# Softcap attention and spectral mixing: who issues the transfers that move squares between partitions

## Chip, cores and metric

The kernel runs on one core of one Trainium2 chip. The metric is the device time of one execution in microseconds; lower is better. Several executions are timed and their median is told. One more execution was recorded by the hardware profiler; every row below is from that one.

## The reference, cut to what matters

```python
scores = scale * np.matmul(q, k.transpose(0, 1, 3, 2))      # 8 batches, 12 heads, 448 x 64
scores = cap * np.tanh(scores / cap)
attn = softmax(scores)                                      # with 1e-09 added to the sum
x = (attn @ v) laid out as [8, 448, 768]

theta = x @ w_theta
zr, zi = x * np.cos(theta), x * np.sin(theta)
y = einsum('ts,bsd->btd', w_tok_r, zr) + einsum('ts,bsd->btd', w_tok_i, zi)
u = x + y
return u + np.maximum(u @ w_ch, 0.0)
```

The theta product and the last product sum over the 768 channels, and the product with `w_tok` sums over the 448 tokens. TensorE sums over partitions, so between the first and the second of them the values `zr` and `zi` must be turned round: channels stand on partitions before, tokens after.

## The kernel before, in words

All work is laid out by hand. `pipeline` runs one script of short words per attention stage `s` (two pairs of heads each, three stages per batch), and each word calls one function. The scripts `FRONT`, `PARTS` and `OTHER` fix the order on every engine; nothing is reordered later, and each engine works through its own instructions in that order. The attention of a batch runs beside the spectral part of the batch before it. A batch `b` of the spectral part takes the three scripts of `PARTS` (a first, a second and a third script); the last batch is finished by scripts of its own in `OTHER`, where no attention is left.

Products that need float32 accuracy are made of three TensorE products in a shorter format: a value is split into a high part (a cast on ScalarE, ACT) and a low part (a subtraction on VectorE, DVE). For the mixing over tokens these are `z_high` (word `h`, L502, writes `zh`) and `z_low` (word `l`, L509, writes `zl`); `mix` (word `M`, L519 to L521, writes `mx`) multiplies them.

The turning is done in two steps. `flip` (word `f`, L481) transposes 32x32 blocks in place of their partitions on DVE and writes a tile `f`, which in the trace is called `g_row` where it lies in a fixed row of memory. `carry` (word `D`, L485 to L493) then moves blocks between partitions with sixteen transfers of 32 partitions x 448 values, 56 KB each, from `f` to a new tile `t`. There are three carries a batch, D0, D1 and D2, each for two of the six channel blocks. D0 and D1 stand in the first script and D2 in the second, in this order of words (cut):

```
... f0 f1 D0 N d2 e2 T3 y3 Pa0 S3 Pb0 q1 t3 e3 d3 a1a a1b sc1 T4 y4 d4 T5 y5 d5 r2 r3 f2 f3 D1
... h0a l0a h0b l0b W h1a ... M0a l1a r4 h1b M0b r5 l1b f4 f5 D2 e0 h2a M1a l2a e1 M1b h2b l2b m0 I ...
    ... M3a h4a l4a M3b h4b l4b Pa0 m2 w2 S3 q1 t3 M4a ...
```

The first word that reads D0's tile is `h0a`, D1's is `h2a`, D2's is `h4a` (in the script `... u0 e2 u1 a0b M3a h4a l4a M3b h4b l4b ...`); the product of the last is `M4a`. A `z_high` reads columns from all four column blocks of `t` and all partitions, so it waits for all sixteen transfers of its carry.

Two things tie the carries together. In the batches with full scripts the tile `f` has one fixed room (`FLIP = (1,)`), so the flips for D2 (`f4 f5`) may not write before D1's sixteen transfers have read it and ended. And the transfers are issued by two engines' queues: SyncE (SP), whose queue also loads `q` and `k` (L232), broadcasts the reciprocal sums (word `I`, `bc`, L407) and stores the output, and GpSimd (POOL), which in this part of the program does nothing else.

Which engine issues what is the line that the change touches; `d` is one of the four column blocks of `t`, `m` one of the four groups of 32 partitions, and `b` counts the batches from 0.

Of the kernel before, what the change touches and what calls it, by code (L numbers as in the profile page):

```python
# [75 lines left out]
def softcap_attn_then_spectral_mix(ctx, tc, qk2, v, cap, w_theta, w_tok, w_ch, outT):  # L76
    nc = tc.nc
    B, NP, P, _, S = qk2.shape
# [406 lines left out]
    def carry(b, i):  # L485

        Z[b, i, "t"] = large.take([P, 4 * S], F32, f"t{b}_{i}")
        f, t = Z[b, i, "f"], Z[b, i, "t"]
        for m in range(4):
            for d in range(4):  # L490
                queue = nc.gpsimd if (b < B - 1 or i) and d == 3 else nc.sync
                queue.dma_start(t[32 * m : 32 * m + 32, d * S : (d + 1) * S], f[32 * d : 32 * d + 32, m * S : (m + 1) * S])  # L492
        large.give(Z.pop((b, i, "f")))  # L493

# [70 lines left out]
    def pipeline(general):  # L565
# [5 lines left out]
        def run(s, b, word):  # L571
# [44 lines left out]
            elif word == "v":  # L616
                if live:
                    load_v(s)
            elif name == "q":
                for part in range(2):  # L620
                    if s + 1 < WHOLE or s + 1 == WHOLE and (i, part) != (1, 1):
                        load_raw(2 * s + 2 + i, part)
            elif word == "Pa1":
                prep_q(2 * s + 1)
            elif word == "Pb1":
                prep_k(2 * s + 1)
            elif word == "Pa0":
                prep_q(2 * s + 2)
            elif word == "Pb0":
                prep_k(2 * s + 2)  # L630
            elif name == "w":
                weights(WEIGHTS.get((s, i), ""))
            elif name == "u":
                split_x(b, i, "us")
            elif name == "X":
                if b + 1 < B:
                    split_x(b + 1, i, "xs")
            elif name == "Y":
                split_x(b, i, "xs")
            elif name in ("h", "l", "M"):  # L640
                {"h": z_high, "l": z_low, "M": mix}[name](b, i, half)
            else:
                {"T": theta, "y": turns, "d": reduce, "sc": sincos, "r": rotate, "f": flip, "D": carry, "m": mix_out, "C": chan,
                 "c": chan_out}[name](b, i)
# [70 lines left out]
```

## Time and profile before

| | |
|---|---|
| Timed, median of 3 runs | 909.82 us (907.93 to 910.62) |
| Profiled execution, its time | 907.38 us |
| Profiled execution, its span | 905.5 us |
| PE (TensorE products) busy | 892.0 us, 99% of the span |
| DVE busy | 657.3 us, 73% |
| ACT busy | 572.3 us, 63% |
| POOL busy | 53.1 us, 6% |
| Carry transfers issued by SP in the line changed | 292 |
| Carry transfers issued by POOL in the line changed | 92 |

The span is the time from the first to the last instruction; the execution's own time is 1.9 us more. Busy shares are means over the whole span; PE's busy time is made of overlapping pipelined products, so even at 99% single waits can lie between them. A chain of waits shows, step by step, what released the work that ended last.

### The profile page before, as it was taken

How to read it: one execution, taken by the hardware profiler on the slowest of the kernel's cores; microseconds unless marked ns; L12 is line 12 of the kernel's file. 1: busy time of each engine (PE TensorE's matmuls, PEld its weight loads, DVE VectorE, ACT ScalarE, POOL GpSimd, SP SyncE). 2: the span in 40 equal slices, each digit the busy share in tenths (PEclk: the TensorE clock that was granted, in tenths of full speed). 3: DMA queues.
4: the chain of work that ended last, by engine and by line, in shares of the span. 5: the costliest groups of instructions: out<-in, count | busy, mean ns of one | idle time of the engine just before them, and what ended most of it. 6: DMA issues, size and time to landing. Idle time of an engine off the chain costs nothing.

```text
span 905.5 us, 13212 instructions
## 1 busy us (share of the span) xinstructions
PE 892.0 (99%) x4896; PEld 638.5 (71%) x4896; DVE 657.3 (73%) x1095; ACT 572.3 (63%) x633; POOL 53.1 (6%) x109
## 2 busy tenths in 40 slices
PE   8999999999999999999999999999999999999997
PEld 4235575757758668677686686776876867779996
DVE  6899859969866598675985678855986659765741
ACT  6887865569845597547965488545894459733420
POOL 0000111100100011000100000000010000100100
PEclk9999999999999999999999999999999999999999
DMA  7653373442423325222442233333242331410411
GB/s 267 203 187 86 101 176 108 149 130 55 123 71 93 92 56 158 63 82 72 105 120 66 79 89 114 82 92 92 71 120 55 112 92 52 110 44 25 111 40 64
DMA packets 51947, 90.70 MB, mean 100 GB/s; under 512 B 10913, under 2 KB 44833, under 8 KB 51873
## 3 DMA queue, kind: packets, MB, share of 16 engines
q1 hardware_dynamic: 44592, 69.21, 26.8%
q0 software_dynamic: 3824, 9.61, 4.0%
q10 hardware_dynamic: 3456, 10.95, 3.9%
q8 instruction: 40, 0.66, 0.3%
q14 instruction: 35, 0.28, 0.1%
HBM read 45.68 MB, written 11.01 MB: 63 GB/s over the span
## 4 chain that ended last, share of the span: by engine, by line
PE 72%; DVE 16%; SPq 3%; issue 3%; DMA 3%; ACT 3%; DVEq 0%; ACTq 0%
PE s L278 11%; PE a L362 10%; PE ch L431 7%; PE ch L433 6%; PE ch L432 6%; PE mx L521 5%; PE th L431 5%; PE mx L519 4%; PE th L432 4%; PE mx L520 4%; PE th L433 4%; PE r L389 3%; SPq L492 3%; DVE g_row L481 2%; DMA t<-g_row 2%
## 5 line engine op out<-in xcount | busy, mean ns | idle before, releaser
L305 ACT ACTIVATE p<-s,qscale 128x1792 f32<-128x1792 f32 (+1 forms) x77 | 117.0, 1520 | 102.9 <-PE s L278 93.3
L519 PE MATMUL mx<-wtk_h,zh 128*128 128x448 f32 x336 | 125.1, 372 | 3.9 <-ACT zh L502 3.9
L521 PE MATMUL mx<-wtk_h,zl 128*128 128x448 f32 x336 | 123.9, 369 | 1.0 <-DVE zl L509 0.6
L520 PE MATMUL mx<-wtk_l,zh 128*128 128x448 f32 x336 | 123.0, 366 | 0.0
L318 ACT ACTIVATE p<-p,cap_sb 128x1792 f32<-128x1792 f32 (+1 forms) x77 | 119.9, 1559 | 2.6 <-PE a L362 1.9
L431 PE MATMUL th<-xs,wth_h 128*128 128x448 f32 x288 | 107.5, 373 | 0.0
L431 PE MATMUL ch<-us,wch_h 128*128 128x448 f32 x288 | 107.4, 373 | 0.0
L432 PE MATMUL th<-xs,wth_h 128*128 128x448 f32 x288 | 105.5, 366 | 0.0
L433 PE MATMUL ch<-us,wch_l 128*128 128x448 f32 x288 | 105.5, 366 | 0.0
L432 PE MATMUL ch<-us,wch_h 128*128 128x448 f32 x288 | 105.3, 366 | 0.0
L433 PE MATMUL th<-xs,wth_l 128*128 128x448 f32 x288 | 105.3, 365 | 0.0
L362 PE MATMUL a<-p,v 128*64 128x448 f32 x496 | 102.6, 545 | 0.0
L362 PEld LDWEIGHTS a<-p,v 128*64 128x64 f32 x496 | 33.1, 136 | 63.9 <-issue 62.5
L519 PEld LDWEIGHTS mx<-wtk_h,zh 128*128 128x128 f32 x336 | 63.1, 188 | 19.1 <-ACT zh L502 7.4
L492 POOL DMA_DIRECT2D t<-g_row x76 | 38.5, 513 | 588.8 <-DVE x_row L414 156.7
L502 ACT CAST zh<-t 128x512 fp32r<-128x512 f32 x84 | 44.6, 560 | 41.6 <-DMA t<-g_row 12.4
L521 PEld LDWEIGHTS mx<-wtk_h,zl 128*128 128x128 f32 x336 | 63.1, 188 | 9.6 <-DVE zl L509 4.4
L520 PEld LDWEIGHTS mx<-wtk_l,zh 128*128 128x128 f32 x336 | 63.1, 188 | 5.1
L431 PEld LDWEIGHTS th<-xs,wth_h 128*128 128x128 f32 x288 | 54.1, 188 | 14.2 <-issue 5.1
L431 PEld LDWEIGHTS ch<-us,wch_h 128*128 128x128 f32 x288 | 54.1, 188 | 13.6 <-issue 2.9
L509 DVE TENSOR_TENSOR zl<-t,zh 128x512 fp32r<-128x512 f32 x84 | 50.1, 616 | 16.7 <-ACT zh L502 9.4
L535 DVE SCALAR_TENSOR_TENSOR x<-ch,x 128x448 f32<-128x448 f32 x43 | 26.7, 622 | 48.3 <-PE ch L433 48.3
(517 smaller groups left out, 1563.5 us busy)
## 6 DMA issues: line engine op xcount, KB each, us to landing
t<-g_row SPq DMA_DIRECT2D x228, 56.0 KB, 2.0
k<-in_qk SPq DMA_DIRECT2D x47, 224.0 KB, 3.4
v<-in_v ACTq DMA_DIRECT2D x23, 448.0 KB, 3.3
out_dram<-x SPq DMA_DIRECT2D x43, 224.0 KB, 1.9
q<-in_qk SPq DMA_DIRECT2D x42, 224.0 KB, 2.8
bc<-ri SPq DMA_DIRECT2D x68, 112.0 KB, 2.3
t<-g_row POOLq DMA_DIRECT2D x76, 56.0 KB, 2.1
x_row<-ri SPq DMA_DIRECT2D x24, 112.0 KB, 2.3
```

The source lines that it names most:

```text
L278: nc.tensor.matmul(out[:, h, :S], kk[rows], qq[rows], start=m == 0, stop=m == len(products) - 1)
L305: nc.scalar.activation(pp, spt.pop((s, n))[:, :m, :, :S], AF.Tanh, scale=qscale)
L318: nc.scalar.activation(pp, pp, AF.Exp, scale=cap_sb)
L362: nc.tensor.matmul(acc_of["a", s, i][h * D : (h + 1) * D, :S], vt[s][:, 6 * i + 3 * h + c, :], U[s, (i, c)][:, h, :], start=first and c == ...
L431: nc.tensor.matmul(acc[:, :S], wh[:, j, ms], t[:, 0, :], start=j == 0, stop=False)
L432: nc.tensor.matmul(acc[:, :S], wh[:, j, ms], t[:, 1, :], start=False, stop=False)
L433: nc.tensor.matmul(acc[:, :S], wl[:, j, ms], t[:, 0, :], start=False, stop=j == NJ - 1)
L492: queue.dma_start(t[32 * m : 32 * m + 32, d * S : (d + 1) * S], f[32 * d : 32 * d + 32, m * S : (m + 1) * S])
L509: nc.vector.tensor_tensor(zl, tokens(b, j)[:, c0:c1], zh.bitcast(F32), op=ALU.subtract)
L519: nc.tensor.matmul(acc[:, :S], zh, wtk_h[:, c, :], start=c == 0, stop=False)
L520: nc.tensor.matmul(acc[:, :S], zh, wtk_l[:, c, :], start=False, stop=False)
L521: nc.tensor.matmul(acc[:, :S], zl, wtk_h[:, c, :], start=False, stop=c == NC2 - 1)
```

## The change

From the second batch on (`b` of 1 and above) POOL issues the transfers with `d` of 2 and 3 instead of those with `d` of 3 alone. Eight of the sixteen transfers of a carry then go through POOL's queue and eight through SP's, where it was four and twelve. The first batch stays as it was (four and twelve), and so does the first carry of the last batch (all sixteen on SP). It is 20 carries of the 24 and 80 transfers that change their queue. What is moved, and from where to where, stays.

```diff
-                queue = nc.gpsimd if (b < B - 1 or i) and d == 3 else nc.sync
+                queue = nc.gpsimd if (b < B - 1 or i) and d >= (2 if b else 3) else nc.sync
```

In SP's queue in the second batch (names `t_0`, `t_1`, `t_2` are the tiles of D0, D1 and D2; `bc` the broadcasts, `q`, `k` and `x_row` loads) the order around the carries is this:

```order
-L492 DMA t_0_1743<-g_row 32x448 x12
+L492 DMA t_0_1743<-g_row 32x448 x8
 L232 DMA k_1804<-in_qk 128x448
-L492 DMA t_1_1871<-g_row 32x448 x12
+L492 DMA t_1_1871<-g_row 32x448 x8
 L232 DMA q_1956<-in_qk 128x448
 L232 DMA x_row<-in_qk 128x448
 L232 DMA k_1963<-in_qk 128x448
-L492 DMA t_2_1995<-g_row 32x448 x12
+L492 DMA t_2_1995<-g_row 32x448 x8
 L407 DMA bc_0_2046<-ri_2041 64x448 x2
 L407 DMA bc_1_2049<-ri_2041 64x448 x2
```

Each group of twelve became eight, and what stands behind it in the queue is the same. In POOL's queue the same three carries, and those of the third batch, stand after one another; this is the order of the changed kernel:

```order
L135 DMA swc5b_raw<-in_wch 128x768
L492 DMA t_0_1743<-g_row 32x448 x8
L492 DMA t_1_1871<-g_row 32x448 x8
L492 DMA t_2_1995<-g_row 32x448 x8
L492 DMA t_0_2668<-g_row 32x448 x8
L492 DMA t_1_2796<-g_row 32x448 x8
L492 DMA t_2_2920<-g_row 32x448 x8
```

Where it read x4 it reads x8, and nothing stands between the carries. On ACT, the first cast that reads D2's tile in the second batch waits for the semaphores of the transfers (DMAHW those of SP and ACT, DMASW those of POOL):

```order
-L502 CAST zh_1915<-t_2_1995 128x512 [waits DMAHW2_49,DMAHW1_49,DMAHW3_49,DMAHW0_49,DMAHW4_49,DMASW7_49,DMAHW5_49,DMASW2_49,DMAHW6_49,DMASW1_49,DMAHW7_49,DMASW0_49,PE_49]
+L502 CAST zh_1915<-t_2_1995 128x512 [waits DMAHW0_49,DMASW7_49,DMAHW1_49,DMASW6_49,DMAHW2_49,DMASW5_49,DMAHW3_49,DMASW4_49,DMAHW4_49,DMASW3_49,DMAHW5_49,DMASW2_49,DMAHW6_49,DMASW1_49,DMAHW7_49,DMASW0_49,PE_49]
```

It waited for twelve DMA semaphores and now for sixteen. On PE, DVE and ACT no instruction is added, taken away or moved.

## Rows read from the trace of the kernel before

**Rows 1.** The page, first part: busy time, share of the span, instructions.

```profile
PE 892.0 (99%) x4896; PEld 638.5 (71%) x4896; DVE 657.3 (73%) x1095; ACT 572.3 (63%) x633; POOL 53.1 (6%) x109
```

**Rows 2.** Busy time by stretch: length, PE, PEld, DVE, ACT, POOL; clock; DMA share; GB/s.

```profile
214.06:322.64 108.58, 107.28 (x596) 79.30 (x596) 78.25 (x127) 71.36 (x79) 6.19 (x12) 1.00 0.32 90
322.64:429.63 106.99, 106.99 (x596) 79.39 (x597) 78.23 (x127) 71.52 (x79) 6.12 (x12) 1.00 0.33 91
429.63:537.57 107.94, 107.57 (x596) 79.23 (x598) 78.11 (x127) 71.32 (x79) 6.12 (x12) 1.00 0.33 90
537.57:645.70 108.13, 107.37 (x596) 79.28 (x598) 78.23 (x127) 71.33 (x79) 6.00 (x12) 1.00 0.32 90
645.70:754.34 108.64, 107.30 (x596) 79.31 (x597) 78.02 (x127) 71.41 (x79) 5.91 (x12) 1.00 0.32 90
822.00:899.72 77.72, 77.72 (x382) 71.55 (x382) 39.49 (x63) 23.33 (x37) 3.92 (x8) 1.00 0.22 61
```

**Rows 3.** PE's timeline at D2's first product, second and third batch: start, length.

```profile
251.37 0.37 PE L278 MATMUL s<-q17l,k17h 64*128 64x448 f32 x2
252.98 0.47 PE L519 MATMUL mx<-wtk_h,zh 128*128 128x448 f32 x1 [1.25 <-ACT zh L502]
...
359.93 0.38 PE L278 MATMUL s<-q23l,k23h 64*128 64x448 f32 x2
360.24 0.47 PE L519 MATMUL mx<-wtk_h,zh 128*128 128x448 f32 x1
```

**Rows 4.** ACT's timeline: casts of D0, D1, D2 (second batch), D2 (third).

```profile
226.78 1.54 ACT L502 CAST zh<-t 128x512 fp32r<-128x512 f32 x3
...
239.55 0.62 ACT L502 CAST zh<-t 128x512 fp32r<-128x512 f32 x1 [1.24 <-DMA t<-g_row]
...
252.31 1.03 ACT L502 CAST zh<-t 128x512 fp32r<-128x512 f32 x2 [4.81 <-DMA t<-g_row]
...
359.05 1.04 ACT L502 CAST zh<-t 128x512 fp32r<-128x512 f32 x2 [2.98 <-DMA t<-g_row]
```

**Rows 5.** SP's queue, second batch, D0, D1, D2: start, time over the group.

```profile
214.06 8.02 SPq L492 DMA_DIRECT2D t<-g_row  x12
...
230.13 7.49 SPq L492 DMA_DIRECT2D t<-g_row  x12
...
241.82 8.77 SPq L492 DMA_DIRECT2D t<-g_row  x12
```

**Rows 6.** L492 by queue: issue ns min/median/max; landing us min/median/max (SP, then POOL).

```profile
L492 SPq DMA_DIRECT2D t<-g_row x228: 507/588/1642, 214.1 to 863.2; - x114
L492 POOL DMA_DIRECT2D t<-g_row x76: 496/496/716, 214.7 to 858.5; - x76
DMA to landing us min/median/max: 1.9/2.0/5.4
DMA to landing us min/median/max: 1.8/2.1/4.5
```

**Rows 7.** Waits of DVE, 205 to 800 us; then its timeline, second batch.

```profile
DVE g_row L481 <- DMA t<-g_row: 14.9, 6, 2.9
...
239.58 2.10 DVE L481 STREAM_TRANSPOSE g_row<-z 128x896 f32<-128x896 f32 x2 [2.37 <-DMA t<-g_row]
...
249.59 1.08 DVE L342 TENSOR_TENSOR ps<-ps,g_row 64x896 f32<-64x896 f32 x1
252.96 1.16 DVE L509 TENSOR_TENSOR zl<-t,zh 128x512 fp32r<-128x512 f32 x2 [2.29 <-DMA bc<-ri]
```

**Rows 8.** POOL's timeline at D1 of the second batch.

```profile
230.68 0.50 POOL L492 DMA_DIRECT2D t<-g_row  x1 [13.84 <-DVE g_row L481]
231.47 1.62 POOL L492 DMA_DIRECT2D t<-g_row  x3 [0.29 <-issue]
```

**Rows 9.** Busy time by stretch (columns as in rows 2), while D1 is issued.

```profile
338.63:346.10 7.47, 7.47 (x46) 5.88 (x42) 6.05 (x10) 7.43 (x7) 1.98 (x4) 1.00 0.59 170
```

**Rows 10.** Semaphore waits ahead of L502, 214 to 800 us: ns min/median/max.

```profile
L502 ACTq EVENT_SEMAPHORE  x144: 17/38/3785, 223.8 to 794.6; - x144
```

## The prediction, made before the changed kernel ran

> **What bounds the kernel now.** I read the busy shares first [rows 1]: PE is busy 892.0 us, 99% of the span, every other engine under 75%. So time can only be won where PE waits, and the change touches no PE instruction. Next I cut the span into the steady batches, each from the first transfer of its D0 to that of the next batch, and compared them [rows 2]. The second to the sixth batch hold the same work (596 products each), but they last 108.58, 106.99, 107.94, 108.13 and 108.64 us. In the third (106.99) PE is never idle; in the others it idles 1.30, 0.37, 0.76 and 1.34 us. That is the reading to learn here: one batch shows what the schedule costs without waits, and what the others take more is 1.59 + 0.95 + 1.14 + 1.65 = 5.33 us.
>
> Who is waited for? In the second batch the last score product starts at 251.37 and the first mixing product of D2's tile at 252.98, 1.61 us later, with a wait for ACT's cast of `zh`; in the third batch the same two stand 0.31 us apart [rows 3]. So PE stood 1.30 us for the cast that reads D2. ACT started that cast at 252.31 after 4.81 us of idleness that ended with a landing; in the third batch it idled 2.98 us at the same place [rows 4]. The cast waits for the last of D2's sixteen transfers. SP took 8.77 us to issue its twelve there, from 241.82 on [rows 5]; POOL has only four.
>
> One step further back, DVE idles 14.9 us in six times before a flip, for landings [rows 7]: D2's flip starts at 239.58 after 2.37 us of waiting, because it overwrites the tile that D1's transfers read. D1's twelve on SP ran from 230.13 over 7.49 us [rows 5], so the last was issued near 230.13 + 7.49 - 0.59 = 237.03 and landed about 2.0 us later [rows 6], at 239.0; ACT's cast of D1 (239.55) and the flip (239.58) follow [rows 4, 7]. So two carries lie in series on this path, D1 and then D2, and SP's issuing is most of each.
>
> **The change, part by part.** *SP loses four transfers per carry.* Twelve took 7.49 us [rows 5], 0.624 us each. With eight the last is issued 7 x 0.624 = 4.4 us after the first instead of 6.9, and lands at +6.4 instead of +8.9 us.
>
> *POOL gains four.* It starts 0.55 us after SP (230.68 against 230.13) [rows 5, 8]. Its interval is (1.62 - 0.50) / 2 = 0.56 us within the three, and (231.47 + 1.62 - 230.68 - 0.50) / 3 = 0.64 with the pause of 0.29 us [rows 8]. The eighth is issued at 0.55 + 7 x 0.56 to 0.64, that is +4.5 to +5.0 us, and with the median landing of 2.1 us [rows 6] is there at +6.6 to +7.1. POOL does nothing else in these batches, so nothing queues behind.
>
> *Sixteen transfers in a shorter time.* While D1 is issued the DMA engines are busy 0.59 of 7.47 us [rows 9], which is 4.4 us of work; squeezed into 5.0 us that is 0.88. No row shows the landing at that load. The bounds are the median, 2.1 us, and POOL's longest, 4.5 us [rows 6], with which the carry is complete at 4.5 + 4.5 = +9.0, no earlier than now. I take +7.2 for D1 and +6.7 for D2, nearer to the median, because most transfers are issued off that peak: D1 lands 1.7 us earlier, D2 takes 2.2 us less.
>
> *What follows.* D2's flip was waiting 2.37 us [rows 7], so it moves up by all of the 1.7 us. D2's transfers then start 1.7 us earlier and take 2.2 us less: the cast may start 3.9 us earlier. ACT has 4.81 us of idleness before it [rows 4], so nothing holds it. DVE's subtraction for the same product starts at 252.96 after 2.29 us of idleness; the work before it ends at 249.59 + 1.08 = 250.67 [rows 7], and earlier flips only pull that forward. PE's wait was 1.30 us, so both are in time with a microsecond or more to spare. Next late at that place is PE itself.
>
> *More waits.* ACT's cast and DVE's flip now wait for sixteen DMA semaphores and not twelve. A wait takes 38 ns [rows 10], so 0.15 us on engines that sit idle there: nothing on the path. If that cover were gone it would be 0.15 us in each of two carries a batch, 2 us over seven.
>
> *Places without gain.* D0's cast starts at 226.78 with no idle time before it [rows 4], some 3 us after the last landing (214.06 + 8.02 - 0.59 + 2.0 = 223.5) [rows 5, 6]; ACT's own order hides D0. In the last batch PE is busy all 77.72 us from 822.00 on [rows 2], so D1 and D2 there win nothing. The first batch is unchanged. The seventh runs into other scripts and has no twin to compare it with; I count nothing for it.
>
> **The sum**, against the profiled execution of 907.4 us: four batches come down to the third one's length, 907.4 - 5.3 = 902.1 us. The timed runs have a median of 909.8, 2.4 us above the profiled one. Waits of this kind vary from batch to batch (0 to 1.65 us), so part of those 2.4 us may be of this kind and go too. I add a third: **902.8 us**, 0.8% less than the median.
>
> **A page against the rows.** SP's issuing is 7.49 us and a landing 2.0 us [rows 5, 6]: here the issuing is the long part. The Trainium skill, "DMA: Bandwidth & Descriptors", section "Issuing engines are not separate DMA queues", says that issuing from several engines only saves the sequencer's issue time, "which is usually small relative to the DMA itself". By that rule the change would bring next to nothing, about 907 to 910 us; these rows speak against the word small here.
>
> **Rivals.**
> *No measurable difference.* The transfers hold each other up: sixteen at a load of 0.88 land so much later that a carry ends as before. It needs landings of 8.9 - 4.5 = 4.4 us for POOL's last, against a median of 2.1 and a longest of 4.5; for it speaks that SP landed one as late as 5.4 [rows 6]. Then the flip and the cast stay where they are: 907.4 to 909.8 us. Halfway, with landings near 4.0 us, each carry gains 0.4 and the two 0.8 us of the 0.95 to 1.65 in four batches: 3.2 us, 904.2 us.
>
> *Slower: POOL becomes the late queue.* With eight to issue, POOL decides as soon as its interval is over (8.9 - 2.1 - 0.55) / 7 = 0.9 us. At 1.0 us instead of 0.56 to 0.64 a carry lands at 0.55 + 7.0 + 2.1 = +9.6, 0.7 us later than now; D1 and D2 add up to 1.4 us per batch. In the third batch the product would follow the cast by 252.98 - 252.31 = 0.67 us, at 359.05 + 0.67 = 359.7, and PE came at 360.24 [rows 3, 4], so 0.5 us are spare there. Second, fourth to sixth and seventh batch lose 1.4 us and the third 0.9: 7.9 us, 915 to 918 us. Against it: none of POOL's 76 transfers took over 716 ns to issue [rows 6]. What could do it is DVE holding GpSimd off for whole instructions of about 1.1 us. The Trainium skill, "SBUF — State Buffer", section "SBUF: two separate sides", states such a trap: GpSimd writes the descriptors of its transfers itself and is locked out while VectorE runs some copies. By that rule this rival is what would happen; the median landing of POOL's transfers, 0.1 us above SP's, shows little of it.
>
> **How the numbers follow.** About 0.3%, 2.7 us, is what a measurement of this kernel can tell from no change. The forecast (PE's waits for D2 gone, 900.8 to 905.5) has 0.71, no difference through crowded transfers 0.13, half gains (up to 907.5) 0.07, a late POOL 0.09. Faster is the forecast and most half gains, 0.76; same 0.15; slower 0.09. The range goes from 900.5, the sum with a microsecond and a half of room, to 908.0, which takes in the half gains and the start of the second case.
>
> **What will show it.** Right, if SP's groups at L492 read x8 and about 5 us and POOL's x8 and 4 to 5 us; if DVE's wait at the flip and ACT's before the D2 cast shrink by about 2 and 4 us; if PE's wait for `zh` in the steady batches is gone; and if all five of them last about 107.0 us. Wrong, if POOL's group takes over 6 us, if landings grow to 4 us and more, or if PE waits elsewhere in those batches.

## The result, and the profile after

The changed kernel takes 901.17 us (median of 6 runs, 900.24 to 901.78), the kernel before 907.88 us beside it (6 runs, 906.68 to 910.62): 0.9919 of the time, with an interval of 0.9906 to 0.9933. The forecast was 902.8 us. The profiled execution took 901.09 us with a span of 899.2, 6.3 us less than before.

The first line of the page, and the first line of the chain that ended last, after and then before:

```profile
PE 889.7 (99%) x4896; PEld 639.2 (71%) x4896; DVE 657.6 (73%) x1095; ACT 572.4 (64%) x633; POOL 92.0 (10%) x189
...
PE 93%; DVE 3%; ACT 1%; issue 1%; DMA 1%; SPq 0%; ACTq 0%
```

```profile
PE 72%; DVE 16%; SPq 3%; issue 3%; DMA 3%; ACT 3%; DVEq 0%; ACTq 0%
```

POOL's busy time grew from 53.1 us [rows 1] by 38.9, which is 80 transfers of 0.49 us; nothing else moved by more than 2.3. The chain runs over PE for 93% of the span, where it was 72%, and SP's queue, at 3% before, has no share in it worth a per cent.

The busy times by stretch, from the first transfer of a batch's D0 to that of the next (columns as in [rows 2]: length, PE, PEld, DVE, ACT, POOL, clock, DMA share, GB/s); the sixth row is the seventh batch:

```profile
213.57:320.55 106.98, 106.98 (x596) 79.39 (x596) 78.33 (x127) 71.45 (x79) 11.89 (x24) 1.00 0.32 91
320.55:427.56 107.01, 107.01 (x596) 79.41 (x598) 78.16 (x127) 71.33 (x79) 11.97 (x24) 1.00 0.32 91
427.56:534.54 106.98, 106.98 (x596) 79.39 (x598) 78.06 (x127) 71.43 (x79) 11.79 (x24) 1.00 0.33 91
534.54:641.55 107.01, 107.01 (x596) 79.35 (x598) 78.16 (x127) 71.30 (x79) 11.97 (x24) 1.00 0.31 91
641.55:748.51 106.96, 106.96 (x596) 79.40 (x597) 78.17 (x127) 71.32 (x79) 11.98 (x24) 1.00 0.32 91
748.51:828.97 80.46, 80.46 (x427) 63.06 (x428) 58.45 (x94) 48.94 (x64) 11.88 (x24) 1.00 0.24 64
```

In all six length and PE are equal: PE never waits. The five steady batches together go from 540.28 us [rows 2] to 534.94, which is 5.34 us less. The seventh batch, from the first transfer of its D0 to that of the eighth, goes from 81.23 to 80.46 us, 0.77 less. What lies ahead of the second batch's D0 is 0.49 shorter (213.57 against 214.06), the end from the eighth batch's D0 on 0.30 longer. The sum is 6.30 us, the whole difference of the spans.

The place where PE waited, D2's first product in the second batch [rows 3], and ACT's casts of D1 and D2 and DVE's flip there [rows 4, 7]; three timelines, of PE, ACT and DVE:

```profile
250.89 0.37 PE L278 MATMUL s<-q17l,k17h 64*128 64x448 f32 x2
251.19 0.47 PE L519 MATMUL mx<-wtk_h,zh 128*128 128x448 f32 x1
```

```profile
236.05 1.79 ACT L318 ACTIVATE p<-p,cap_sb 128x1792 f32<-128x1792 f32 x1
237.96 0.62 ACT L502 CAST zh<-t 128x512 fp32r<-128x512 f32 x1
...
248.25 1.03 ACT L502 CAST zh<-t 128x512 fp32r<-128x512 f32 x2 [1.22 <-PE mx L521]
```

```profile
238.09 2.10 DVE L481 STREAM_TRANSPOSE g_row<-z 128x896 f32<-128x896 f32 x2 [1.35 <-DMA x_row<-in_qk]
```

The product follows the score product after 0.30 us, where it was 1.61 [rows 3]. ACT's cast of D2 starts 2.9 us ahead of it. Its row names PE as what ended the wait, but D2's last transfer landed at 247.92, 0.33 us before the cast, much as before (251.94 and 252.31), so the landing may still be what it waits for. D1's cast has no idle time in brackets: it follows the work before it on ACT. The flip still waits for transfers, 1.35 us instead of 2.37 [rows 7]. Its row names a load (`x_row`), yet it starts 0.6 us after D1's last landing as it did before (238.09 after 237.48, 239.58 after 239.01), and still does in a run below that moves those loads away (238.84 after 238.23).

SP's and POOL's queues in the same batch (D0, D1, D2):

```profile
213.57 4.99 SPq L492 DMA_DIRECT2D t<-g_row  x8
...
229.64 4.96 SPq L492 DMA_DIRECT2D t<-g_row  x8
...
240.33 6.02 SPq L492 DMA_DIRECT2D t<-g_row  x8
```

```profile
214.24 4.12 POOL L492 DMA_DIRECT2D t<-g_row  x8 [44.71 <-PE s L278]
230.17 0.50 POOL L492 DMA_DIRECT2D t<-g_row  x1 [11.81 <-DVE g_row L481]
230.87 3.42 POOL L492 DMA_DIRECT2D t<-g_row  x7 [0.20 <-issue]
240.86 4.01 POOL L492 DMA_DIRECT2D t<-g_row  x8 [6.57 <-DVE zl L509]
```

SP's twelve took 8.02, 7.49 and 8.77 us [rows 5]; its eight take 4.99, 4.96 and 6.02. POOL's interval within D1's seven is (3.42 - 0.50) / 6 = 0.49 us, and its eighth goes out at 230.87 + 2.92 - 229.64 = +4.15 us from SP's first.

The transfers of L492 by queue over the whole span, landing us (min/median/max), SP and then POOL:

```profile
DMA to landing us min/median/max: 1.9/2.6/5.4
DMA to landing us min/median/max: 1.8/2.3/5.0
```

The median landing rose from 2.0 to 2.6 us on SP and from 2.1 to 2.3 on POOL [rows 6]: the crowding is real, but small beside the issuing that was saved.

### The profile page after: what moved, and what is told of

Read it like the earlier page. It is cut to its first block, busy times and chain, and to the rows that moved or that the text cites. A ratio compares the mean times of both kernels' runs of the same rounds, so it can differ in the third digit from the quotient of the medians.

```text
span 899.2 us, 13310 instructions
## 1 busy us (share of the span) xinstructions
PE 889.7 (99%) x4896; PEld 639.2 (71%) x4896; DVE 657.6 (73%) x1095; ACT 572.4 (64%) x633; POOL 92.0 (10%) x189
## 4 chain that ended last, share of the span: by engine, by line
PE 93%; DVE 3%; ACT 1%; issue 1%; DMA 1%; SPq 0%; ACTq 0%
PE s L278 15%; PE a L362 12%; PE mx L519 7%; PE mx L520 7%; PE th L431 7%; PE mx L521 7%; PE ch L431 7%; PE th L432 7%; PE th L433 7%; PE ch L433 6%; PE ch L432 6%; PE r L389 4%; PE a L355 2%; ACT p L305 1%; DVE wch_l L161 0%
## 5 line engine op out<-in xcount | busy, mean ns | idle before, releaser
L492 POOL DMA_DIRECT2D t<-g_row x152 | 75.4, 503 | 544.4 <-DVE x L414 153.0
L461 DVE SCALAR_TENSOR_TENSOR z<-z 128x448 f32<-128x448 f32 x48 | 29.7, 619 | 42.0 <-ACT z L456 41.9
```

## The experiments

The theory: PE waits for the last transfer of D2, behind D1 and D2 in series, and SP's issuing is most of each. Its rivals: that transfers hold each other up, that POOL becomes late, and that the gain comes from SP's queue being free sooner for its loads. All kernels are the changed kernel with one edit or two, and ratios are to the kernel before, run on the same chip. "D1 at +7.9" means: its last transfer lands 7.9 us after its first was issued, computed from the trace's issue and completion records.

**One carry at a time.** The three runs split every carry but one as before. The line is shown against the kernel before:

```diff
-                queue = nc.gpsimd if (b < B - 1 or i) and d >= (2 if b else 3) else nc.sync
+                queue = nc.gpsimd if (b < B - 1 or i) and d >= (2 if b and i == 0 else 3) else nc.sync
```

This is for D0 alone; the other two have `i == 1` (D1) and `i == 2` (D2).

> Eight and eight for D0 alone, from the second batch on; D1 and D2 as before (twelve and four). My theory (PE waits for D2, which waits for D1 and D2 in series, and D0 lands 3 us before it is read): no difference, ratio 0.998 to 1.002, second to sixth batch together 538 to 542 us as before. Rival (what counts is SP's queue being free earlier for the loads and broadcasts behind every carry): a third of the gain, ratio 0.997 or less.

> Eight and eight for D1 alone. Theory: D1 lands about 1.1 us earlier, D2's flip and with it all of D2 moves up by as much, so most of the 1.3 us waits go: 902 to 904 us, ratio 0.993 to 0.996; PE idle in the five steady batches together 0 to 1 us where it was 3.8. Rival (D1 is hidden, only D2's own issuing counts): ratio 0.998 to 1.002.

> Eight and eight for D2 alone. Theory: D2's own issuing is 2.3 us shorter, more than the longest wait of 1.3 us, so nearly the whole gain: 901 to 902.5 us, ratio 0.991 to 0.994; PE not idle in the steady batches. Rival (the gain is the sum of shares of the three carries): a third to a half of the gain, ratio 0.995 to 0.997.

D0 alone: 907.36 us, ratio 1.0002 (0.9989 to 1.0014), no change. D1 alone: 902.78, ratio 0.9938 (0.9919 to 0.9958). D2 alone: 902.94, ratio 0.9944 (0.9927 to 0.9962). The five batches by stretch with D0 alone:

```profile
213.56:321.61 108.05, 107.29 (x596) 79.32 (x596) 78.25 (x127) 71.42 (x79) 7.99 (x16) 1.00 0.32 90
321.61:428.60 106.99, 106.99 (x596) 79.42 (x598) 78.25 (x127) 71.55 (x79) 8.06 (x16) 1.00 0.33 91
428.60:536.84 108.24, 107.58 (x596) 79.23 (x596) 78.21 (x127) 71.32 (x79) 8.08 (x16) 1.00 0.33 90
536.84:644.15 107.31, 107.29 (x596) 79.28 (x598) 78.12 (x127) 71.43 (x79) 7.89 (x16) 1.00 0.32 91
644.15:752.45 108.30, 107.29 (x596) 79.31 (x596) 78.22 (x127) 71.34 (x79) 7.96 (x16) 1.00 0.32 90
```

PE still idles 0.66 to 1.01 us in three of the five and 0.02 in a fourth, although SP is done with D0 sooner. The five are 1.4 us shorter together than before [rows 2]; but D2, which is split as before, landed sooner in the two that shrank most (in the fifth at +9.3 instead of +9.8), so this share can't be told from the scatter of single transfers. Nor does the ratio settle it, because the end after the last product is 7.4 us long in this execution and 5.4 before (more on that under the edges). So the rival falls for the bulk of the gain, which does not come with D0; whether D0 brings a microsecond of it is open. With D1 alone the five last 107.27, 106.99, 106.99, 108.07 and 106.96 us; with D2 alone 106.98, 106.98, 107.28, 107.01 and 106.97. The five shrink by 4.0 us with D1 alone and by 5.1 with D2 alone, of the 5.3 with all three. Either carry is enough in most batches, so the gains of the two (4.3 and 4.1 us against 907.04) don't add: they shorten one chain whose excess is at most 1.7 us a batch. The 902.94 of D2 alone lies above the 901 to 902.5 that were expected; its end after the last product is 7.0 us long, 5.5 with D1 alone, so its batches gained more than its median shows. D1 alone left 1.07 us in the fifth batch, where one of SP's twelve transfers of D2 took 2.30 us to issue and the last landing came at +10.6; D2 alone left 0.3 in the fourth.

**Four, eight, twelve, sixteen.** One number in the same condition sets how many of the sixteen POOL takes from the second batch on: `d >= (4 if b else 3)` none, `d >= (1 if b else 3)` twelve, `d >= (0 if b else 3)` all; the last batch's D0 stays on SP.

> From the second batch on all sixteen transfers on SP, none on POOL. Theory (SP's issue interval of 0.62 us is the price): D1 lands 2.5 us later than before, D2's flip 2.5 us and D2's landing 5.0 us later; PE's wait grows by about 5 us in six batches (4.5 in the third): 930 to 942 us. Rival (the time is in the landings and not in the issuing): under 915 us.

All sixteen on SP: 943.11 us, ratio 1.0403 (1.0374 to 1.0432), a little more than expected. SP's queue for D1 and D2, then PE's waits from 205 to 860 us (total, times, longest):

```profile
228.84 10.01 SPq L492 DMA_DIRECT2D t<-g_row  x16
...
243.01 11.25 SPq L492 DMA_DIRECT2D t<-g_row  x16
```

```profile
PE mx L519 <- ACT zh L502: 14.7, 12, 4.2
PE mx L521 <- DVE zl L509: 8.4, 6, 1.5
```

Each four transfers more on SP cost 2.5 us of issuing, (10.01 - 0.59) / 15 = 0.63 each, and the products that read D1 and D2 now wait. This is the theory driven the other way, at 36 us instead of the 6.7 of the first step, since nothing is spare any longer. But not all of the 36 us are waits. PE's wait for D2 in the second batch, and then two stretches of that batch, before the wait and after it (columns as in [rows 2]):

```profile
256.62 0.58 PE L519 MATMUL mx<-wtk_h,zh 128*128 128x448 f32 x1 [4.23 <-ACT zh L502]
```

```profile
250.00:252.00 2.00, 2.00 (x12) 1.59 (x12) 1.56 (x2) 0.00 (x0) 0.00 (x0) 1.00 0.41 97
258.00:260.00 2.00, 2.00 (x7) 1.78 (x6) 1.93 (x5) 0.96 (x2) 0.00 (x0) 0.50 0.44 122
```

After PE had stood idle for 4.23 us the granted clock was 0.50, that is 1.2 GHz instead of 2.4, and PE did seven products in 2 us instead of twelve. This lasted 3.41 us, and it happens once in each of the six batches. It costs about half of that time, 1.7 us each or 10 us in all (an estimate from these rows). In the profiled execution PE's idle time from the second batch on grew by 21 us and its busy time, for the same products, by 11. With all on POOL, below, it happens twice, and in the kernels before and after the change not once from the second batch on, until the last product is done. So more than a quarter of the 36 us is what the slower clock took on top of the waits.

> From the second batch on twelve transfers on POOL and four on SP. Theory (a carry ends when the longer queue has issued, and POOL's interval is 0.49 us): POOL's twelfth goes out at 0.55 + 11 x 0.49 = 5.9 us and lands at +8.2 to +9.5, close to before: 903 to 908 us, PE idle in the steady batches 0 to 4 us. Rival (POOL's descriptors are held up by DVE, so that long series of its transfers take 0.9 us each or more): over 915 us.

Twelve on POOL: 913.83 us, ratio 1.0070 (1.0052 to 1.0087): slower than the theory's 903 to 908, and short of the rival's 915. SP's queue at D1, POOL's, and the transfers issued from 336 to 352 us (D1 of the third batch: KB each, median us to landing):

```profile
229.97 2.56 SPq L492 DMA_DIRECT2D t<-g_row  x4
232.57 0.58 SPq L232 DMA_DIRECT2D q<-in_qk  x1
233.20 0.45 SPq L232 DMA_DIRECT2D x_row<-in_qk  x1
233.69 0.44 SPq L232 DMA_DIRECT2D k<-in_qk  x1
```

```profile
230.50 5.88 POOL L492 DMA_DIRECT2D t<-g_row  x12 [9.70 <-DVE g_row L481]
```

```profile
t<-g_row POOLq DMA_DIRECT2D x12, 56.0 KB, 4.2
v<-in_v ACTq DMA_DIRECT2D x1, 448.0 KB, 3.3
t<-g_row SPq DMA_DIRECT2D x4, 56.0 KB, 3.5
```

POOL is no slower: (5.88 - 0.50) / 11 = 0.49 us. But SP is done after 2.56 us and sends its three loads of 224 KB into the middle of POOL's twelve, whose median landing here is 4.2 us. D1 is complete at +9.3 to +10.6 us in the five batches, later than the +8.8 to +9.5 before the change, and all five last 108.9 to 109.6 us. A new theory: the queue that is freed early collides.

> From the second batch on all sixteen on POOL. Theory: the sixteenth goes out at 0.55 + 15 x 0.49 = 7.9 us and lands at +10.2 to +11.5, 1.3 to 2.5 us later than before in D1 and again in D2: PE waits 3 to 5 us more in six batches, 925 to 938 us, and less than with all on SP. Rival (POOL held up by DVE or by a full ring): POOL's group takes over 12 us and the time is over 950 us.

All on POOL: 921.65 us, ratio 1.0149 (1.0133 to 1.0165), less than expected. POOL's queue for D1:

```profile
230.00 7.91 POOL L492 DMA_DIRECT2D t<-g_row  x16 [7.75 <-DVE g_row L481]
```

Sixteen in a row keep the interval of 0.49 us. D1 is there at +9.1 to +9.9 us, sooner than with twelve: SP, with no transfers of its own, sent its three loads at 213.8 to 214.7 us, beside D0, so none collides with D1. So POOL alone is a better queue for this than SP alone by 21 us (some 7 of them the clock, as above), and two are better than one.

**Is it the loads?** Two kernels hold SP's three loads (`load_raw` with part 1) back until the word `S2` of the script, behind D2: one with eight and eight, one with twelve on POOL.

```diff
     def load_raw(k, part):
+        if state.get("hold"): return state["late"].append((k, part))
...
+                if word == "S2" and state["hold"]:
+                    state["hold"] = False
+                    [load_raw(*late) for late in state["late"]]
```

> The changed kernel (eight and eight), but in the second script of the second to seventh batch SP's three loads behind D1 (two of q, one of k) are issued after D2 and the broadcasts. Theory now: it is these loads, 672 KB that go out as soon as SP has issued its eight, that made D1 land at +7.3 to +9.0 us where the median landings gave +6.6 to +7.1; without them D1 lands at +6.4 to +7.3 us. PE had no wait left, so the time stays within 1 us of the changed kernel's. Rival (sixteen transfers in a shorter time, or the load of v, slow each other): D1 lands as late as before, over +7.3 us.

> Twelve transfers on POOL and four on SP, with the same three loads behind D2 and the broadcasts. Theory now: the kernel with twelve on POOL was slow because SP, done after 2 us, sent its loads into POOL's transfers; without them D1 lands at +8.2 to +8.8 us instead of +9.3 to +10.6 and the time falls from 914 to 902 to 907 us. Rival (a series of twelve on POOL is slow of itself, held up by DVE or by its own descriptors): D1 lands at +9.3 us or later and the time stays over 911 us.

With eight and eight nothing changes: 901.63 us, ratio 0.9924 (0.9904 to 0.9945), D1 at +7.27 to +8.96 us against +7.30 to +8.98 without the move. My theory for that kernel falls: these loads did not hold D1 up there. With twelve on POOL the move brings 913.83 down to 903.95 us, ratio 0.9957 (0.9942 to 0.9972). POOL's twelve as above in that kernel (336 to 345.5 us):

```profile
t<-g_row POOLq DMA_DIRECT2D x12, 56.0 KB, 1.8
```

POOL's landings fall from 4.2 to 1.8 us, D1 to +7.7 to +8.8, and PE's waits for its casts and subtractions (205 to 860 us) from 7.1 us to 0.4. So of the 12.7 us that twelve cost against eight and eight, 10 were the collision with SP's loads. Of the 2.8 us that are left, 1.2 stand in the five batches, where D2 lands at +9.1 to +9.9 us (+8.9 to +9.9 without the move, +6.4 to +7.7 with eight and eight), and 1.3 in a longer end after the last product.

**Or the load of v?** One more transfer goes out with D1: ACT's of `v`, 448 KB. The word `v` of the second script was moved from D1 to D2.

```diff
-cV0 cV1 v sc2 Pa1 S1 Pb1 q0 t1 M0a
+cV0 cV1 sc2 Pa1 S1 Pb1 q0 t1 M0a
...
-S2 t2 M2a h3a l3a m1
+S2 v t2 M2a h3a l3a m1
```

> The changed kernel (eight and eight), but from the second to the seventh batch ACT's load of v (448 KB), which went out just before D1, goes out after the cast that reads D1, beside D2; SP's loads stay where they were. Theory now: it is this load that held D1's landings up. D1 lands at +6.4 to +7.0 us instead of +7.3 to +9.0, D2 up to 1.5 us later than its +6.4 to +7.7; PE has room for both, so the time stays within 1 us of the changed kernel's. Rival (D1's sixteen transfers hold each other up, or SP's loads of q and k do): D1 lands at +7.3 us or later as before.

900.44 us, ratio 0.9915 (0.989 to 0.994). The issues from 336 to 344 us (D1, third batch), of the changed kernel and of this one:

```profile
v<-in_v ACTq DMA_DIRECT2D x1, 448.0 KB, 3.1
t<-g_row SPq DMA_DIRECT2D x8, 56.0 KB, 3.7
t<-g_row POOLq DMA_DIRECT2D x8, 56.0 KB, 3.4
```

```profile
t<-g_row SPq DMA_DIRECT2D x8, 56.0 KB, 2.3
t<-g_row POOLq DMA_DIRECT2D x8, 56.0 KB, 2.1
v<-in_v ACTq DMA_DIRECT2D x1, 448.0 KB, 4.1
```

Without `v` beside it D1 lands 1.2 us earlier, at +6.5 to +7.5 (mean 6.76 over the five batches, against 7.92). The share of time that the DMA engines are busy while SP issues D1 of the third batch falls from 0.79 to 0.53. So it was this load that stretched D1's landings. The steady batches stay at 107.0 us, as PE waited nowhere in them.

**The edges.** `d >= 2` in place of `d >= (2 if b else 3)` splits the first batch too; `nc.gpsimd if d >= 2` also the last batch's D0; and one kernel has the first batch's split and the late `v`.

> Eight and eight in the first batch as well (not in the first carry of the last). Theory: in the changed kernel PE still waits 0.5 us for a low part in the first batch, so at most 0.7 us is to be had: 900.3 to 901.5 us, no difference to the changed kernel. Rival (the loads of the last weights stand behind these transfers in POOL's queue and come later): 1 to 4 us slower than the changed kernel, with PE waiting for channel products after the first batch.

> Eight and eight in all 24 carries, the last batch's first one too. Theory: PE has no wait in the last batch, so its first carry being 5 us shorter gives nothing: as the run with the first batch, within 1 us. Rival (the last batch's D0 delays D1 and D2 behind it on SP and these the end): 1 to 4 us faster.

> Both helpful edits at once: eight and eight in the first batch too, and the 448 KB load of v issued beside D2. Theory: the steady batches already last 107.0 us, where PE never waits, so an earlier D1 buys nothing in them; what the late v won alone (0.7 us) was a wait in the first batch that the split there removes too. The two do not add: median 898.8 to 899.8 us, five steady batches of 106.95 to 107.02 us, a first batch (D0 to D0) of 114.2 to 114.5 us, D1 landing at +6.5 to +7.5 us. Rival: the slack won at D1 is worth something in the seventh batch or in the timed executions, whose waits vary; then the two add to about 898.5 us or less, and the seventh stretch is shorter than 80.46 us by over 0.3 us.

The first: 899.26 us, ratio 0.9907 (0.9893 to 0.9921). The first batch, D0 to D0, of the changed kernel and of this one:

```profile
97.40:213.57 116.17, 114.92 (x631) 76.73 (x629) 92.59 (x178) 75.42 (x89) 12.28 (x23) 1.00 0.44 127
```

```profile
97.33:211.74 114.41, 114.41 (x631) 76.81 (x629) 92.50 (x178) 75.53 (x89) 18.04 (x35) 1.00 0.43 129
```

It shrinks by 1.8 us to PE's own work. (Kernels with the first batch unchanged spread from 115.5 to 117.1 us there.) I had expected at most 0.7 from the one wait at 143 us and overlooked that a score product at 166 us waited too; that wait of 0.7 us went with the same edit. The last batch's D0 on POOL adds nothing: 901.39 us, ratio 0.9929 (0.9916 to 0.9942), with the same batches. Its end is longer, 7.5 us from the last product to the end of the span against 5.5 in the first. It can't be put down to the edit: D0 alone, D2 alone and both kernels with twelve on POOL end 7.0 to 7.5 us after the last product too, the other nine kernels 5.4 to 5.8. No engine's work fills the difference; SP stands 1.4 to 2.1 us between two of its last semaphore instructions, and why is open. So kernels whose medians differ by 2 us or less are better compared by their batches. The two helpful edits together don't add: 899.63 us, ratio 0.9906 (0.9893 to 0.992), first batch 114.37 us. The late `v` had nothing left to remove: it leaves the first batch's code as it was, and the 0.7 us by which it alone came out below the changed kernel stand in that batch (115.48 against 116.18 us), inside its spread. The intervals of these three kernels overlap that of the changed kernel, so against it the traces show the 1.8 us, not the ratios.

## Why the prediction came out right

*The wait and its chain.* Right, and shown from both sides: either of D1 and D2 sped up removes most of PE's waits, all on SP costs 36 us, and D0 alone brings nothing that can be told from scatter. The sum said 5.33 us from five batches; they gave 5.34.

*The size.* From the profiled execution the sum was 5.3 us, and 6.3 came. Two terms were zero that aren't. The seventh batch gave 0.77 us; its 427 products before held 81.10 us of PE's busy time, now 80.46, so that a wait was hidden in "busy" and the row looked unwaited but for 0.14 us. And 0.49 us came ahead of the second batch's D0, where no code differs; other kernels with the same first batch spread from 115.5 to 117.1 us there, so this is its own scatter, and its sign was luck. The third of 2.4 us that I added for the gap between profile and median was not there: three more runs put the median before at 907.88 us, beside its profiled 907.4. (902.1 and a third of 2.4 are 902.9, not 902.8; the tenth matters nowhere.) The two add up: the predicted 902.8 stands 1.6 us above the measured median, 1.0 for the gains that I didn't count and the rest for what I added.

*SP's term.* 4.4 us to the last issue was predicted; (4.96 - 0.59) = 4.37 measured.

*POOL's term.* Mis-sized: an interval of 0.56 to 0.64 us read from three and four transfers; it is 0.49 in long groups, and the pause comes once. The eighth goes out at about +4.15, not +4.5 to +5.0. So POOL did not decide, as I had taken it to: in the second to the sixth batch the last landing of D1 and of D2 is one of SP's each time.

*Crowding.* Mis-sized for D1: +7.2 was taken, +7.3 to +9.0 measured (mean 7.92), although POOL issued sooner. The load was right: 0.88 was worked out, and the DMA engines were busy 0.79 to 0.94 while SP issued D1 in the five batches. But I took most landings to stay near the median, and left out what else is sent with the sixteen. The run with the late `v` gives +6.76, so the 1.2 us between are that load. For D2, +6.7 was taken and +6.4 to +7.7 measured.

*What follows.* The flip moved up by 1.0 us in the second batch (from SP's first transfer of D1 to that of D2: 11.7 before, 10.7 after; over five batches 1.1), not by 1.7, because D1 came later than I took; its wait shrank by 1.0 us, half of the sign that I had set. D2's cast moved up by 22.18 - 18.61 = 3.6 us from the start of D1, against 3.9. The slack of a microsecond and more absorbed both errors.

*The rivals.* Crowding as far as no gain needed landings of 4.4 us: single ones come to 5.4, but the medians are 2.6 and 2.3. A late POOL needed an interval of 0.9 us: it is 0.49, and still 0.49 over sixteen, with DVE busy in 73% of the span. The page "SBUF — State Buffer" of the Trainium skill (section "SBUF: two separate sides") describes GpSimd locked out while VectorE copies; with eight, twelve or sixteen on POOL none of its carry transfers took over 723 ns to issue, and in the changed kernel its median landing, 2.3 us, is below SP's 2.6, so no run here shows it. The slower outcome existed at twelve, but through another mechanism than mine: the loads behind SP's shortened group.

*The rule of the Trainium skill.* "DMA: Bandwidth & Descriptors" of the Trainium skill (section "Issuing engines are not separate DMA queues") calls the issue time "usually small relative to the DMA itself". Here it was the larger part: from none to four to eight transfers on a second queue, 943.11, 907.88 and 901.17 us. Its other half, that all transfers interleave on the same DMA engines whoever issues them, fits what twelve on POOL and the load of `v` showed: landings grew with what other queues sent beside them.

## What to carry to other kernels

Cut the span at a repeating mark and compare like stretches: the best one shows what the work costs, and the excess of the others bounds what a change in waits can give. When many small transfers end in one wait, price the issuing queue first (0.62 us on SP and 0.49 us on POOL against landings of 2 us here) and split them so that both queues finish together. Then look at what stands behind the shortened queue and beside it on others: the loads that come forward can cost more than the split brings, and moving them is as cheap as the split.

## What the runs showed of the hardware

SP's transfers, normally 0.59 us to issue, now and then take 1.0 to 2.3 us (one of 1.65 us in the group of D2 above, 6.02 us for eight), whether eight, twelve or sixteen per carry. They come together with the loading of instructions: over all fourteen traces 87 of the 88 transfers of L492 on SP that took more than 1 us started within 0.6 us of the start of a 16 KB packet of the queue that the profile calls `q8 instruction` (in the group above the packet starts at 243.7 us and the slow transfer at 244.06). How the one brings the other was not tried. A 448 KB load beside sixteen transfers of 56 KB lengthened their median landing from 2.1 and 2.3 us to 3.4 and 3.7 (POOL and SP, D1 of the third batch). POOL's issue interval stayed at 0.49 us over seven, twelve and sixteen in a row. With all on SP the granted clock fell to 0.50 (1.2 GHz) for 3.41 us in each of six batches, after PE had waited 4.23 and 2.63 us in two of them, and in the other four 0.2 to 1.0 us and then 1.4 to 1.5.
